# A new order of batch loads in a fused sparse-attention and feed-forward kernel

## The chip, the core and the metric

The kernel runs on one core of a Trainium2 chip. The metric is the device time of one execution in microseconds. Before the change it is 222.42 us, the median of three runs (220.64 to 222.76). Less is better. A result counts as faster or slower here if it differs by over 2%.

Five engines work side by side: TensorE (PE, matmuls, with its weight loads listed apart as PEld), VectorE (DVE), ScalarE (ACT), GpSimd (POOL) and SyncE (SP). In this kernel GpSimd issues the loads that change the type from f32 to bf16 or f16, and SyncE issues the stores and the transposes made by DMA. Matmul results lie in PSUM, everything else on chip in SBUF.

## The reference

Two parts, one after the other. The first is attention with 4 batches, 8 heads, 768 positions and head size 64. Each query sees the keys within 15 positions of it (`window`), and one summary for each block of 32 positions: the maximum of the block's keys, with the mean of its values.

```python
k_sum = k.reshape(B, H, nb, block, D).max(axis=3)
v_sum = v.reshape(B, H, nb, block, D).mean(axis=3)
scores_l = scale * np.matmul(q, k.transpose(0, 1, 3, 2))     # kept where |i - j| < 16
scores_s = scale * np.einsum('bhsd,bhnd->bhsn', q, k_sum) + np.log(block)
# softmax over both kinds of scores together: a
attn = np.matmul(a, np.concatenate([v, v_sum], axis=2))
# ... (cut: mask, softmax)
x = attn.transpose(0, 2, 1, 3).reshape(B * S, H * D)          # 3072 x 512
h = x @ w_in                                                  # 512 x 2048
out = (h / (1.0 + np.exp(-1.702 * h))) @ w_out                # 2048 x 512
```

## The kernel before

The feed-forward part is cut into eight *units* of 384 rows, two for each batch: unit u holds half u % 2 of batch u // 2. A unit has an *input stage* (`ff_in`: 16 tiles `nt` of 4 matmuls each, then the gelu on ScalarE) and an *output stage*. Units 0 and 1 have an output stage of their own (`ff_out`). Units 2 and 3, 4 and 5, 6 and 7 are taken as pairs: two input stages, then one output stage for both, in which the products `a`, `b`, `c` with parts 1 to 7 save one multiplication in eight. The attention of the next batch is slipped in between these matmuls.

The helpers that matter here (cuts are marked):

```python
def load_kc(b):                       # load_qc(b) is the same for q
    rows["k", b] = rows_tile("k", b)  # tile kb, or for batch 2 a half of kq; queries: qb, kq
    cast_load(k, b, rows["k", b])     # 8 DMAs on GpSimd's queue, one a head

def load_vc(b):                       # vw[b % 2] is used by every second batch
    w5 = vw[b % 2].rearrange("p (j e) h c -> p j e h c", e=2)
    for j in range(NJ):               # NJ = 6 DMAs on GpSimd's queue
        pool.dma_start(out=w5[:, j, 0, :, 0:D], in_=...)

def v_odd(b): ...                     # VectorE: 4 copies of the value rows within vw
def vsum(s, js): ...                  # 24 matmuls ps_vs<-vw,E: sums over value blocks
def block_sums(): ...                 # VectorE: 4 copies vs<-ps_vs
def halo_dmas(w5, j0): ...            # 4 DMAs vw<-vw on GpSimd's queue: neighbours' rows
def sum_dmas(w5, j0, eng=pool): ...   # 2 DMAs vw<-vs: the block sums to each tile

def tk(p, s):                         # keys of batch 1, two heads: transposed on TensorE
    ps = trans(rows["k", 1][:, p].rearrange("p j h d -> p j (h d)"))   # 6 matmuls ps_t<-ident,kb
    copy(act if p % 2 else dve, at(flat_kx(p, s), 0, [[256, NJ], [192, 2], [1, 64]]),
         ps.rearrange("p (j e c) -> p j e c", e=2, c=64))
    ks = attp.tile([128, nb], BF16, name="ks", tag="ks")
    dve.tensor_reduce(out=ks, in_=ps.rearrange("p (n s) -> p n s", s=block),
                      axis=AX.X, op=ALU.max)
    key_halos(p, s)
    key_rows(p, s, ks)

def xk(g, b): ...                     # SyncE: 2 DMA transposes, keys of 4 heads, batches 2 and 3
def xq(g, b): ...                     # SyncE: 1 DMA transpose, queries of 4 heads, batches 2 and 3
def dx(g, m): ...                     # SyncE: 1 DMA transpose xT<-x of an attention result
```

The transposes and block sums (`ps_t`, `ps_vs`), and also the scores `ps_s`, share one PSUM pool of two buffers. The pool `mm` of four banks holds the rest.

Units 0 and 1 (their input stages, and what is put beside them):

```python
for u in range(2):
    todo = {}
    if u == 0:
        # ... (cut: casts of the queries of batch 0)
    else:
        def value_rows():
            vsum(1, range(NJ))
            block_sums()
            halo_dmas(w51, 0)
            sum_dmas(w51, 0)
            load_kc(2)
            load_qc(2)
            load_vc(2)

        todo = {1: [lambda: tk(0, 1)], 2: [lambda: v_odd(1)], 4: [lambda: tk(1, 1)],
                6: [value_rows, lambda: tk(2, 1)], 8: [lambda: tk(3, 1)]}
        ff_in(u, range(3))
    for nt in range(0 if u else N0, NT):
        if u == 0 or nt > 2:
            ff_in(u, (nt,))
        for f in todo.get(nt, ()):
            f()
    exp_soon()
    if u == 0:
        beside(1, -1)
        load_qc(1)
        busy(6)
    # ... (cut: order of the output stage)
    for i, (ms, part) in enumerate(order):
        ff_out(u, ms, part)
        beside(u + 1, i)              # attention of the next half batch
        # ... (cut)
        if u == 1 and i == 3:
            for g in range(2):
                xk(g, 2)
```

The pairs of units, with what is put into their input stages (`first` for unit 2b, `second` for unit 2b + 1):

```python
for b in range(1, B):
    n, s = b + 1, (b + 1) % 2
    more = n < B
    ss = stage.tile([128, NP - 1, 2, NI, 128], F16, name="ss", tag="vf")
    u = 2 * b
    # ... (cut: pairs "a", "b", "c", whose sums go to ss[:, 0], ss[:, 1], ss[:, 2])
    first, second = {}, {0: [lambda: pairs["a"].sums(0, NI)]}
    for nt, i0, i1 in ((7, 0, 4), (13, 4, 7)):
        second[nt] = [lambda i0=i0, i1=i1: pairs["b"].sums(i0, i1),
                      lambda i0=i0, i1=i1: pairs["c"].sums(i0, i1)]
    if b == 1:
        first = {0: [lambda: values(1, 1, 0, True)],
                 2: [lambda: dx(0, 1), lambda: values(1, 1, 1, True)], 4: [lambda: dx(1, 1)]}
    elif more:
        for g in range(2):
            xk(g, n)
    if more:
        first.setdefault(6, []).append(lambda: v_odd(n))
        # ... (cut: rest_k, maxima and halos of the keys of batch n, at nt 3, 5, 8, 10)
        def bring():
            w5 = vw[s].rearrange("p (j e) h c -> p j e h c", e=2)
            vsum(s, range(NJ))
            block_sums()
            halo_dmas(w5, 0)
            sum_dmas(w5, 0)
            if n + 1 < B:
                load_kc(n + 1)
                load_vc(n + 1)
                load_qc(n + 1)

        when = 7 if b == 1 else 14
        first.setdefault(when, []).append(lambda: [xq(g, n) for g in range(2)])
        first.setdefault(9 if b == 1 else 15, []).append(bring)
    for w, todo in ((u, first), (u + 1, second)):
        ff_in(w, range(3))
        # ... (cut: the other tiles, and after each what todo has for it)
    # ... (cut: the output stage of the pair, with the attention of batch n)
```

Batch 0 comes in another way and is over early. Each engine carries out its instructions in the order of the program.

Of the kernel before, what the change touches and what calls it, by code (L numbers as in the profile page):

```python
# [11 lines left out]
F16 = mybir.dt.float16  # L12
# [23 lines left out]
def kernel(  # L36
# [10 lines left out]
    B, H, S, D = q.shape  # L47
# [8 lines left out]
    NJ = S // 128  # L56
# [8 lines left out]
    dve = _Ordered(tc, nc.vector)  # L65
    act = _Ordered(tc, nc.scalar)
    pool = _Ordered(tc, nc.gpsimd)
    sp = _Ordered(tc, nc.sync)

    consts = ctx.enter_context(tc.tile_pool(name="consts", bufs=1))  # L70
# [44 lines left out]
    def cast_load(x, b, dst):  # L115

        for h in range(H):
            pool.dma_start(out=dst[:, h // 2, :, h % 2],
                           in_=x[b, h].rearrange("(j p) d -> p j d", p=128))

    def rows_tile(what, b):
        if b != 2:
            return castp2.tile([128, NP, NJ, 2, D], BF16, name=what + "b", tag=what + "b")
        if "two" not in early:
            early["two"] = stage.tile([128, 2, NP, NJ, 2, D], BF16, name="kq", tag="kf")
        return early["two"][:, "kq".index(what)]

    def load_kc(b):
        rows["k", b] = rows_tile("k", b)
        cast_load(k, b, rows["k", b])  # L130

    def load_qc(b):
        rows["q", b] = rows_tile("q", b)
        cast_load(q, b, rows["q", b])

    def load_vc(b):
        w5 = vw[b % 2].rearrange("p (j e) h c -> p j e h c", e=2)
        for j in range(NJ):
            pool.dma_start(out=w5[:, j, 0, :, 0:D],
                           in_=v[b, :, j * 128:(j + 1) * 128].rearrange("h p d -> p h d"))  # L140

    def v_odd(b):
        for p in range(NP):
            r = rows_of(b % 2, p)
            dve.tensor_copy(out=r[:, :, 1], in_=r[:, :, 0])
# [129 lines left out]
    def copy(eng, out, in_):  # L275
        if eng is act:
            act.activation(out=out, in_=in_, func=ACT.Copy)
        elif eng == "dve_alone":

            dve.tensor_reduce(out=out, in_=in_.unsqueeze(len(in_.shape)), axis=AX.X, op=ALU.max)  # L280
        else:
            eng.tensor_copy(out=out, in_=in_)
# [24 lines left out]
    def rows_of(s, p, hh=None):  # L307

        hs = slice(2 * p, 2 * p + 2) if hh is None else slice(2 * p + hh, 2 * p + hh + 1)
        return vw[s].rearrange("p (j e) h c -> p j e h c", e=2)[:, :, :, hs, 0:D]  # L310
# [24 lines left out]
    def busy(n):  # L335
        ps = pmm.tile([128, 512], F32, name="ps_w", tag="mm")
        for i in range(n):
            pe.matmul(out=ps[:, 0:128], lhsT=warm[:, 0:128], rhs=warm[:, 0:128],
                      start=True, stop=True)
# [8 lines left out]
    def halo_dmas(w5, j0):  # L348
        halo_odd(w5, j0)
        halo_even(w5, j0)  # L350
# [26 lines left out]
    def at(ap, start, dims):  # L377
        a = ap[:, start:start + 1]
        return bass.AP(tensor=a.tensor, offset=a.offset, ap=[a.ap[0]] + dims)

    def flat_kx(p, s):
        return kx[p][s].rearrange("p t c -> p (t c)")
# [182 lines left out]
    def trans(src):  # L565
        big = psb.tile([128, 2048], BF16, name="ps_t", tag="big")
        for j in range(NJ):
            pe.transpose(out=big[:, j * 128:(j + 1) * 128], in_=src[:, j], identity=ident)
        return big[:, 0:S]

    def tk(p, s):
        ps = trans(rows["k", 1][:, p].rearrange("p j h d -> p j (h d)"))
        copy(act if p % 2 else dve, at(flat_kx(p, s), 0, [[256, NJ], [192, 2], [1, 64]]),
             ps.rearrange("p (j e c) -> p j e c", e=2, c=64))
        ks = attp.tile([128, nb], BF16, name="ks", tag="ks")
        dve.tensor_reduce(out=ks, in_=ps.rearrange("p (n s) -> p n s", s=block),
# [3 lines that stand above are left out]
# [221 lines left out]
            self.store(1, 0, True)  # L801

    gate = consts.tile([128, 2], F32, name="gate")
    dve.memset(gate, 0.0)

    def gelu_soon():
# [161 lines left out]
# [3 lines that stand above are left out]
            for p in range(NP):  # L971
                todo.setdefault(12 + p // 2, []).append(lambda p=p: cast_q(dve, p, 1))
# [3 lines that stand above are left out]
                block_sums()  # L976
                halo_dmas(w51, 0)
                sum_dmas(w51, 0)
                load_kc(2)
                load_qc(2)  # L980
                load_vc(2)

            todo = {1: [lambda: tk(0, 1)], 2: [lambda: v_odd(1)], 4: [lambda: tk(1, 1)],
                    6: [value_rows, lambda: tk(2, 1)], 8: [lambda: tk(3, 1)]}
            ff_in(u, range(3))
        for nt in range(0 if u else N0, NT):
            if u == 0 or nt > 2:
# [4 lines that stand above are left out]
        if u == 0:  # L992
            beside(1, -1)
            load_qc(1)
            busy(6)
        order = [(ms, part) for ms in range(JH) for part in range(4)]
        if u == 0:

            order = [(ms, part) for part in range(4) for ms in range(JH)]
        for i, (ms, part) in enumerate(order):  # L1000
            ff_out(u, ms, part)
            beside(u + 1, i)
            if u == 0 and i in (4, 7, 10):
                w_sums(i // 3 - 1)
            if u == 1 and i == 2:
                w_sums(3)
# [3 lines that stand above are left out]
# [19 lines left out]
# [5 lines that stand above are left out]
        pairs = {"a": Pair((u, 0), (u, 1), ss[:, 0], not more),  # L1034
                 "b": Pair((u, 2), (u + 1, 2), ss[:, 1], not more),
                 "c": Pair((u + 1, 0), (u + 1, 1), ss[:, 2], not more)}
# [5 lines that stand above are left out]
            first = {0: [lambda: values(1, 1, 0, True)], 2: [lambda: dx(0, 1), lambda: values(1, 1, 1, True)],  # L1042
                     4: [lambda: dx(1, 1)]}
# [5 lines that stand above are left out]
            at_k = [(first, 3), (first, 5), (first, 8), (first, 10)] if b == 1 else \  # L1049
                [(first, 8), (first, 10), (first, 12), (first, 14)]  # L1050
            for p, (when, nt) in enumerate(at_k):
                when.setdefault(nt, []).append(lambda p=p: rest_k(p, s))
# [4 lines that stand above are left out]
                block_sums()  # L1057
                halo_dmas(w5, 0)
                sum_dmas(w5, 0)
                if n + 1 < B:  # L1060
                    load_kc(n + 1)
                    load_vc(n + 1)
                    load_qc(n + 1)

            when = 7 if b == 1 else 14
            first.setdefault(when, []).append(lambda: [xq(g, n) for g in range(2)])
            first.setdefault(9 if b == 1 else 15, []).append(bring)
        for w, todo in ((u, first), (u + 1, second)):
            ff_in(w, range(3))
            for nt in range(NT):  # L1070
                if nt > 2:
                    ff_in(w, (nt,))
                for f in todo.get(nt, ()):
                    f()
        pairs["a"].p1(act)
        if more:
            exp_soon()
        for m in "bc":
            pairs[m].sums(NI - 1, NI)
        for what in order:  # L1080
            getattr(pairs[what[0]], "p" + what[1])()
            if more:
                for it in meet.get(what, ()):
                    attend(n, it)
# [30 lines left out]
```

## Time and profile before

| | |
|---|---|
| time, median of three runs | 222.42 us (220.64 to 222.76) |
| span of the profiled execution | 222.2 us |
| TensorE busy | 203.3 us, 92% of the span |
| VectorE, ScalarE, GpSimd busy | 133.5, 123.3, 94.0 us |
| loads and copies issued by GpSimd: share of 16 DMA engines over the span | 75.3% |
| DMAs issued by SyncE, same share | 29.7% |
| packets under 512 B | 84480 of 96609 |

How to read it: "PE ps_vs L28 <- DMA vw<-in_v_dram" says that TensorE's instruction writing `ps_vs` waited for a load that writes `vw` from the input `v`. Line 28 is a helper through which every instruction passes, so lines are told apart by their tiles. Here is the part of the page that shows the span in 40 slices of 5.55 us each. A digit is the busy share of an engine in tenths, or the clock granted to TensorE in tenths:

```profile
PE   7779998997999994179999999999999999999994
PEld 2556554555655562036688886655888866568883
DVE  6687936788818774075466776089677740347332
ACT  2675775446675593017782456767824567773220
POOL 8779988698699830049995001022000000000000
PEclk9999999999999999559999999999999999999999
DMA  6999999999999999969999345799013460000223
```

The kernel starts with the first half of batch 0. Units 0 and 1 last until 77.8 us, units 2 and 3 with their pair's output stage until 135, units 4 and 5 until 180, and units 6 and 7 until the end. The sixteenth to eighteenth slices, 83 to 100 us, are in unit 2.

The waits with the largest totals in the stretch from 76 to 114 us are, in us in total, how often, and the longest:

```profile
ACT gT L28 <- PE ph L28: 16.9, 24, 11.4
POOL vw L28 <- DVE vw L28: 16.7, 1, 16.7
PEld L28 <- issue: 12.4, 19, 2.5
DVE vw L28 <- DMA vw<-in_v_dram: 10.0, 1, 10.0
PE ps_vs L28 <- DMA vw<-in_v_dram: 8.9, 5, 2.4
```

### The profile page before, as it was taken

To read this page: it belongs to the slowest core of one execution; us is meant where nothing else is said; L and a number is where in the kernel's file an instruction comes from. 1 tells how busy PE (TensorE), PEld (TensorE's weight loads), DVE (VectorE), ACT (ScalarE), POOL (GpSimd) and SP (SyncE) were. 2 spreads that over 40 slices of the span, in tenths; PEclk is the share of its full clock that TensorE was granted. 3 is DMA by queue.
4 is the path that set the end of the run, shared out by engine and by line. 5 is a ranking of instruction groups with operands and counts; after the bars stand their busy time and mean duration, and the time that the engine had idled before them with its cause. 6 is when DMAs were issued, how large, how long until landed. Compare 5 with 4: busy or idle time off the path is not lost.

```text
span 222.2 us, 5497 instructions
## 1 busy us (share of the span) xinstructions
PE 203.3 (92%) x2193; PEld 137.0 (62%) x2193; DVE 133.5 (60%) x392; ACT 123.3 (55%) x230; POOL 94.0 (42%) x172
## 2 busy tenths in 40 slices
PE   7779998997999994179999999999999999999994
PEld 2556554555655562036688886655888866568883
DVE  6687936788818774075466776089677740347332
ACT  2675775446675593017782456767824567773220
POOL 8779988698699830049995001022000000000000
PEclk9999999999999999559999999999999999999999
DMA  6999999999999999969999345799013460000223
GB/s 181 272 170 182 258 230 214 159 169 213 172 108 153 144 118 207 148 91 145 126 145 149 95 114 176 132 124 165 0 39 97 112 185 1 0 3 24 74 71 118
DMA packets 96609, 29.33 MB, mean 132 GB/s; under 512 B 84480, under 2 KB 93600, under 8 KB 96584
## 3 DMA queue, kind: packets, MB, share of 16 engines
q0 software_dynamic: 67920, 14.88, 75.3%
q1 hardware_dynamic: 28664, 14.11, 29.7%
q8 instruction: 17, 0.28, 0.5%
q14 instruction: 8, 0.07, 0.1%
HBM read 27.26 MB, written 6.29 MB: 151 GB/s over the span
## 4 chain that ended last, share of the span: by engine, by line
PE 57%; DMA 27%; POOL 9%; DVE 2%; issue 1%; SPq 1%; ACT 1%; POOLq 0%
PE ph L28 26%; PE px L28 14%; DMA w_out_sb<-in_moe_w_out_dram 8%; PE pw L28 7%; DMA vw<-in_v_dram 7%; POOL kq L28 4%; DMA kq<-in_q_dram 4%; PE py L28 4%; DMA qb<-in_q_dram 3%; DMA kb<-in_k_dram 3%; POOL qb L28 3%; PE ps_av L28 2%; PE ps_s L28 2%; DMA kf<-in_k_dram 2%; POOL vw L28 1%
## 5 line engine op out<-in xcount | busy, mean ns | idle before, releaser
L28 PE MATMUL ph<-xT,w_in_sb 128*128 128x384 f16 x512 | 87.5, 330 | 0.0
L28 ACT ACTIVATE gT<-ph 128x384 f16<-128x384 f32 x128 | 60.9, 490 | 37.3 <-PE ph L28 37.0
L28 PEld LDWEIGHTS <-w_in_sb 128*128 128x128 f16 x512 | 50.1, 99 | 33.3 <-issue 2.1
L28 PEld LDWEIGHTS <-gT 128*128 128x128 f16 x384 | 35.7, 98 | 12.3
L28 ACT ACTIVATE a_sb<-ps_s 128x768 bf16<-128x768 f32 x28 | 21.2, 806 | 12.0 <-PE ps_s L28 11.9
L28 POOL DMA_DIRECT2D vw<-vw x12 | 6.6, 553 | 43.4 <-DVE vw L28 35.5
L28 PE MATMUL po<-w_out_sb,gT 128*128 128x512 f16 x96 | 23.1, 380 | 0.0
L28 PEld LDWEIGHTS <-ss 128*128 128x128 f16 x216 | 21.0, 98 | 2.5
L28 DVE TENSOR_TENSOR a_sb<-a_sb,mk 128x768 bf16<-128x768 bf16 x28 | 15.5, 554 | 9.9 <-ACT a_sb L28 8.4
L28 DVE TENSOR_TENSOR ss<-gT 128x512 f16<-128x512 f16 (+3 forms) x21 | 8.0, 382 | 21.5 <-ACT gT L28 21.5
L28 ACT ACTIVATE t<-px 128x256 f32<-128x256 f32 x21 | 8.1, 384 | 20.2 <-PE px L28 20.2
L28 PE MATMUL pw<-tb,gT 128*128 128x256 f16 x144 | 18.7, 273 | 0.0
L28 PE MATMUL px<-ta,ss 128*128 128x256 f16 x144 | 18.7, 273 | 0.0
L28 POOL DMA_DIRECT2D vw<-in_v_dram x18 | 16.0, 945 | 2.0 <-DMA kq<-in_q_dram 2.0
L28 DVE TENSOR_TENSOR x<-ps_av,rc 128x384 f16<-128x384 f32 x28 | 15.6, 558 | 1.0
L28 DVE TENSOR_REDUCE ks<-kx 128x24 bf16<-128x768 bf16 x12 | 11.3, 945 | 7.6 <-DMA kx<-kb 7.6
L28 POOL DMA_DIRECT2D kb<-in_k_dram x16 | 13.3, 869 | 2.7 <-DMA w_out_sb<-in_moe_w_out_dram 2.7
L28 ACT ACT_TABLE_LOAD x10 | 12.8, 1283 | 1.0 <-PEq L1099 0.8
L28 POOL DMA_DIRECT2D qb<-in_q_dram x16 | 13.3, 950 | 0.0
L28 DVE TENSOR_TENSOR osb<-pw,t 128x256 f32<-128x256 f32 x18 | 7.6, 423 | 9.2 <-PE pw L28 5.1
L28 PE MATMUL ps_vs<-vw,E 128*32 128x128 bf16 x72 | 2.6, 232 | 8.9 <-DMA vw<-in_v_dram 8.9
L28 DVE COPY vw<-vw 128x768 bf16<-128x768 bf16 x12 | 4.3, 419 | 10.0 <-DMA vw<-in_v_dram 10.0
(103 smaller groups left out, 256.4 us busy)
## 6 DMA issues: line engine op xcount, KB each, us to landing
out_dram<-osb SPq DMA_DIRECT2D x18, 256.0 KB, 3.1
vw<-in_v_dram POOLq DMA_DIRECT2D x18, 128.0 KB, 5.0
w_in_sb<-in_moe_w_in_dram POOLq DMA_DIRECT2D x4, 512.0 KB, 9.5
w_out_sb<-in_moe_w_out_dram POOLq DMA_DIRECT2D x4, 512.0 KB, 17.7
kf<-in_k_dram SPq DMA_DIRECT2D x8, 192.0 KB, 3.7
kb<-in_k_dram POOLq DMA_DIRECT2D x16, 96.0 KB, 5.3
qb<-in_q_dram POOLq DMA_DIRECT2D x16, 96.0 KB, 5.4
out_dram<-osb SPq DMA_DIRECT2D x12, 128.0 KB, 1.7
```

The source lines that it names most:

```text
L28: r = f(*a, **kw)
```

## The change

The loads on GpSimd's queue are put in another order, and the work that needs them in unit 1 as well.

- The keys of batch 2 are issued straight after the queries of batch 1, ahead of the value rows of batch 1 (its halo copies and block sums within `vw`). They no longer stand behind VectorE's work on these values.
- After the value rows of batch 1 come the values of batch 2, and then its queries. Before, it was keys, queries, values.
- In unit 1 the work on the keys and values of batch 1 is set to other tiles: the first two keys ahead of the value copies, the block sums at tile 9 where they were at tile 6. The copies of the transposed keys out of PSUM are all on VectorE, where two of four were on ScalarE.
- The loads of batch 3 follow a small GpSimd copy that reads a part of `ss`, which VectorE writes at tile 7 of unit 3. So they are held until then. Before, they went out once the value rows of batch 2 were issued.

The amount of data loaded and the number of matmuls stay the same.

```diff
--- before.py
+++ after.py
@@ -570,7 +570,7 @@
 
     def tk(p, s):
         ps = trans(rows["k", 1][:, p].rearrange("p j h d -> p j (h d)"))
-        copy(act if p % 2 else dve, at(flat_kx(p, s), 0, [[256, NJ], [192, 2], [1, 64]]),
+        copy(dve, at(flat_kx(p, s), 0, [[256, NJ], [192, 2], [1, 64]]),
              ps.rearrange("p (j e c) -> p j e c", e=2, c=64))
         ks = attp.tile([128, nb], BF16, name="ks", tag="ks")
         dve.tensor_reduce(out=ks, in_=ps.rearrange("p (n s) -> p n s", s=block),
@@ -801,6 +801,7 @@
             self.store(1, 0, True)
 
     gate = consts.tile([128, 2], F32, name="gate")
+    after = consts.tile([128, 2], F16, name="after")
     dve.memset(gate, 0.0)
 
     def gelu_soon():
@@ -976,12 +977,11 @@
                 block_sums()
                 halo_dmas(w51, 0)
                 sum_dmas(w51, 0)
-                load_kc(2)
+                load_vc(2)
                 load_qc(2)
-                load_vc(2)
-
-            todo = {1: [lambda: tk(0, 1)], 2: [lambda: v_odd(1)], 4: [lambda: tk(1, 1)],
-                    6: [value_rows, lambda: tk(2, 1)], 8: [lambda: tk(3, 1)]}
+
+            todo = {0: [lambda: tk(0, 1)], 3: [lambda: tk(1, 1)], 5: [lambda: v_odd(1)],
+                    6: [lambda: tk(2, 1)], 9: [value_rows], 11: [lambda: tk(3, 1)]}
             ff_in(u, range(3))
         for nt in range(0 if u else N0, NT):
             if u == 0 or nt > 2:
@@ -992,6 +992,7 @@
         if u == 0:
             beside(1, -1)
             load_qc(1)
+            load_kc(2)
             busy(6)
         order = [(ms, part) for ms in range(JH) for part in range(4)]
         if u == 0:
@@ -1057,11 +1058,15 @@
                 block_sums()
                 halo_dmas(w5, 0)
                 sum_dmas(w5, 0)
-                if n + 1 < B:
-                    load_kc(n + 1)
-                    load_vc(n + 1)
-                    load_qc(n + 1)
-
+
+            def later():
+                pool.tensor_copy(out=after, in_=ss[:, 2, 0, 0, 0:2])
+                load_kc(n + 1)
+                load_vc(n + 1)
+                load_qc(n + 1)
+
+            if n + 1 < B:
+                second[7].append(later)
             when = 7 if b == 1 else 14
             first.setdefault(when, []).append(lambda: [xq(g, n) for g in range(2)])
             first.setdefault(9 if b == 1 else 15, []).append(bring)
```

## The prediction

> **What bounds the kernel now.** I read the 40 slices of the page first, then the chain of waits from 60 us on, then TensorE's own timeline around the hole that both show, then the stretches with granted clock, then the timelines of VectorE, GpSimd and the sync queue to see why the data came when it did. The chain:
>
> ```profile
> 53.39 7.45 DMA qb<-in_q_dram
> 60.84 0.28 issue
> 61.12 8.95 POOL kq L28 x11
> 70.07 8.58 DMA kq<-in_q_dram
> 78.65 0.30 issue
> 78.95 0.86 POOL vw L28
> 79.81 15.83 DMA vw<-in_v_dram
> 95.64 0.04 issue
> 95.68 0.30 PE ps_vs L28 x4
> 95.98 16.19 PE ph L28 x88
> ```
>
> Start, length, what. From 53 to 95.7 us the end is set by loads alone: queries of batch 1 (qb), keys and queries of batch 2 (kq), then values of batch 2 (vw). From 95.98 the rest of the chain is TensorE without a gap until 218.94, followed by the last addition and store. So whatever is taken out ahead of 95.98 comes off the time, as long as no later wait opens. TensorE's timeline (start, length, instruction, idle before and who ended it):
>
> ```profile
> 80.77 4.72 PE L28 MATMUL ph<-xT,w_in_sb 128*128 128x384 f16 x28
> 85.42 0.24 PE L28 MATMUL ps_vs<-vw,E 128*32 128x128 bf16 x4
> 86.09 0.24 PE L28 MATMUL ps_vs<-vw,E 128*32 128x128 bf16 x4 [0.43 <-DMA vw<-in_v_dram]
> 88.68 0.24 PE L28 MATMUL ps_vs<-vw,E 128*32 128x128 bf16 x4 [2.35 <-DMA vw<-in_v_dram]
> 91.19 0.30 PE L28 MATMUL ps_vs<-vw,E 128*32 128x128 bf16 x4 [2.27 <-DMA vw<-in_v_dram]
> 93.63 0.30 PE L28 MATMUL ps_vs<-vw,E 128*32 128x128 bf16 x4 [2.14 <-DMA vw<-in_v_dram]
> 95.68 0.30 PE L28 MATMUL ps_vs<-vw,E 128*32 128x128 bf16 x4 [1.75 <-DMA vw<-in_v_dram]
> ```
>
> The 24 block-sum matmuls of batch 2 follow the six value loads one by one, 2.0 to 2.6 us apart, from 85.42 to 95.98 us: 10.6 us for work that took 0.52 us for batch 1 (53.90). The stretches (busy us and count of TensorE, its weight loads, VectorE, ScalarE, GpSimd; then clock, DMA share, GB/s) show what comes after the hole:
>
> ```profile
> 85.00:90.00 5.00, 1.14 (x16) 0.41 (x14) 0.95 (x5) 0.86 (x2) 0.00 (x0) 0.93 1.74 179
> 90.00:95.00 5.00, 0.59 (x8) 0.22 (x8) 0.00 (x0) 0.00 (x0) 0.00 (x0) 0.50 1.48 142
> 95.00:100.00 5.00, 4.32 (x19) 2.11 (x19) 4.00 (x14) 1.12 (x3) 2.37 (x5) 0.54 0.58 92
> 100.00:105.00 5.00, 5.00 (x32) 3.01 (x31) 2.78 (x8) 3.56 (x8) 5.00 (x7) 1.00 1.09 143
> ```
>
> The clock is halved from about 89 us and stays so until nearly 100, so the first matmuls after the hole run slowly. A second, small hole:
>
> ```profile
> 55.71 0.49 PE L28 MATMUL ps_t<-ident,kb 128*128 128x128 bf16 x6 [1.29 <-DVE ks L28]
> ```
>
> In unit 1's input stage the third key transpose waits for a PSUM buffer, because VectorE reads the second key's maximum only after four value copies (1.95 us from 52.84).
>
> **What the Trainium skill says.** "TensorE: Matmul & The Clock Gate", Part 1 (The HAM clock gate), says that TensorE's clock drops to half after an idle window of about 3.4 us and comes back after about as long a busy one. The trace agrees: 0.93, 0.50, 0.54, 1.00 above. "DMA: Bandwidth & Descriptors", Issuing engines are not separate DMA queues, says that transfers of all issuing engines run on the same 16 DMA engines and interleave; its section Queues, rings and completion order says each DMA engine takes turns between the queues. The trace agrees: one value load of batch 2 landed every 2.0 to 2.6 us while the sync queue ran transposes and stores; those of batch 3, with the sync queue idle, landed 3.9 to 4.5 us after issues 0.87 us apart.
>
> **The change, part by part.** GpSimd's order of issue was qb(1), value rows(1), k2, q2, v2. It becomes qb(1), k2, value rows(1), v2, q2. ("Value rows" are the four halo copies and two sum copies inside vw.)
>
> *k2.* GpSimd ends qb(1) at 54.37 and then waits for VectorE, issues the six row copies and waits 1.00 us for a landing; k2 goes out from 59.26 to 66.89. Now it starts at 54.4, 8 issues of 0.85 us, the last held to about 61 by the landing of the last qb at 60.84: done at about 62. Its landing (3.3 us after issue) moves from 69.3 to about 65.5.
>
> *Value rows(1).* Issued 62 to about 65.7 (2.27 + 1.38 us as now), landing 3 to 4 us later, 68.5 to 69.5; now 62.8 (58.6 + 4.2). First reader: the value product of batch 1 at 70.27, about 69.1 after the shift below. Touch and go: I put down 0.2 us.
>
> *v2 ahead of q2.* v2 is issued from about 65.7 and takes the place that q2 has now, beside the key transposes. q2's last load was issued at 72.5 and landed 9.4 us later, 81.9. v2 moves the same bytes (6 x 128 KB for 8 x 96 KB) and starts some 1 to 2 us earlier: landed at about 80. It is needed at about 84 (85.42 less the shift). The hole closes: end of the sums 95.98 becomes 85.42 + 0.45, so 10.1 us less.
>
> *Clock.* 64 ph matmuls at full clock took 10.40 us (135.30 in the chain), 0.1625 each. The 88 after the hole took 16.19, at that rate 14.30: 1.9 us less.
>
> *Unit 1.* Keys go in pairs ahead of the value copies, and all four PSUM copies are on VectorE: 2 x 0.56 us more there, 2 x 0.81 less on ScalarE. One key is 0.56 + 0.95 + 0.37 + 0.23 = 2.1 us; four keys, value copies 1.95 and sums 1.17 make 11.5 from 51.1: 62.6 if simply added, about 61.5 with the overlaps that the timeline shows (now 60.4). TensorE's stage is 64 x 0.1625 + 4 x 0.35 + 0.45 = 12.3 from 48.6: 60.9, now 62.2. The 1.29 goes, some 0.2 may come back on the fourth transpose: 1.1 less.
>
> *What opens.* Unit 3 needs xT of batch 1, second half. Its two transposes were issued at 82.0 and 83.4 and landed 7.9 and 8.5 us later (89.9 and 91.9), behind the key transposes and two stores of 10 us; hidden today by the hole. Now unit 3 starts at 77.83 - 1.1 + 10.4 + 0.95 + 0.45 = 88.5, and wants the second xT about 1 us into its first group. With issue 1.1 earlier and a little less traffic they land at about 88.5 and 90.5: 1.0 us of wait.
>
> *q2 last.* It takes v2's place, without the query transposes beside it: landed at about 91. The two qT transposes follow it (7.5 and 7.1 us to landing for batch 3): 95 and about 98. Unit 3 ends at 88.5 + 1.0 + 10.4 = 99.9, and the first score of batch 2 comes two products (1.74) later at 101.6, needing only the first. No wait.
>
> *Batch 3.* The held loads go out from about 95 (after tile nt 7 of unit 3) instead of 101.0, and are done by about 116; batch 3 is first read in the transposes at 138 (about 126 after). Nothing on the path, bar a slower xT transpose or two.
>
> Sum: 10.1 + 1.9 + 1.1 - 0.2 - 1.0 = 11.9 us. From 222.42: 210.5. I add 0.5 for waits that I have not seen: 211.0.
>
> **The rivals.** *Rows late:* k2 ahead of the rows delays batch 1's value product. For it: both sit on one queue and the margin is near zero. Against: the row copies queue up behind nothing but k2, which is nearly through by then; today they are issued behind the whole of qb and still land 4.2 to 6.0 us later. Two more us: 213. *xT wait in full:* if the sync queue is no faster than now, unit 3 waits until 91.9, 2.4 us more than my 1.0 leaves: 213.5. If it waits over 3.4 us the clock falls too and 2 us more go: 215.5. *Query wait:* if q2 is slow in landing, the score at 101.6 waits for its transposes; if they take as long as now (10.9 us) from 91, that is 102, hardly a wait; at 95 it is 4 to 5 us: 215.5. *Only moved:* v2 still late by half: 217. Against it: an earlier issue by some 8 us.
>
> **Range and chances.** The steps that save are read from holes in the trace and are nearly certain; those that cost are 0 to 3 us each and unlikely to come together. The three times before spread by 2.1 us. Range 208.5 to 215.5. Two per cent is below 218.0: it takes two rivals at once to miss it, hence 0.91 faster, 0.07 same, 0.02 slower.
>
> **What would show it.** In TensorE's timeline the six ps_vs groups of batch 2 should be one block of about 0.5 us near 84, with no wait for vw; the clock should be 1.00 throughout 85 to 105; the ps_t wait on DVE ks gone. A wait of about 1 us for xT should stand at the start of unit 3. Wrong if a wait for vw stands at the value product near 69, if a wait of over 2 us stands before ps_s near 101, or if the block sums still wait.

## The result, and the profile after

| | before | after |
|---|---|---|
| time, median | 221.62 us | 212.37 us (211.98 to 213.9) |
| ratio to before | | 0.959, 95% interval 0.952 to 0.967 |
| span of the profiled execution | 222.2 us | 210.6 us |
| TensorE busy | 203.3 us, 92% | 201.3 us, 96% |

The change makes the kernel 4.1% faster. First the slices of the page of the changed kernel, two rows of them, TensorE's busy share and its granted clock:

```profile
PE   7879999999999999989999989999999999999993
PEclk9999999999999999999999999999999999999999
```

The hole of slices 16 to 18 is gone, and with it the two slices at half clock. In place of the hole stand two dents of one tenth. What they are is seen in the chain of waits of the changed kernel (start, length, what):

```profile
79.30 2.60 PE ph L28 x16
81.90 8.32 DMA xT<-x
90.22 0.04 issue
90.27 9.59 PE ph L28 x58
99.85 0.87 PE px L28 x8
```

Before, three loads in a row set the end up to 95.7 us. Now the chain is TensorE's, but for the DMA transpose of an attention result (xT) in unit 3. A second one of the same kind stands in unit 4. TensorE's timeline of the changed kernel:

```profile
83.89 0.52 PE L28 MATMUL ps_vs<-vw,E 128*32 128x128 bf16 x24
84.34 5.05 PE L28 MATMUL ph<-xT,w_in_sb 128*128 128x384 f16 x30
90.27 9.59 PE L28 MATMUL ph<-xT,w_in_sb 128*128 128x384 f16 x58 [0.88 <-DMA xT<-x]
...
124.60 9.59 PE L28 MATMUL ph<-xT,w_in_sb 128*128 128x384 f16 x58 [0.64 <-DMA xT<-x]
```

The 24 block sums are one block of 0.52 us, where they were six groups over 10.6 us. The stretches (busy us and count of TensorE, weight loads, VectorE, ScalarE, GpSimd; clock, DMA share, GB/s) have the clock at 1.00 throughout:

```profile
85.00:90.00 5.00, 4.39 (x28) 2.48 (x26) 4.92 (x19) 2.94 (x6) 2.26 (x4) 1.00 1.82 159
90.00:95.00 5.00, 4.73 (x30) 2.85 (x30) 1.16 (x2) 3.53 (x8) 1.24 (x2) 1.00 1.31 135
95.00:100.00 5.00, 5.00 (x33) 3.11 (x32) 3.14 (x9) 3.72 (x9) 2.78 (x4) 1.00 1.21 121
```

From TensorE's timeline one can read where each stage begins: the first `ph` of an input stage, the first `po` or `px` of an output stage. This table has the lengths of the stages, worked out so for every profile of this study. The stages left out are equal to 0.1 us in all of them (23.13 for the output stage of units 2 and 3, 65.67 from the output stage of units 4 and 5 to the end).

| kernel, lengths in us | unit 1 begins at | unit 1 input | unit 1 output | units 2, 3 input | units 4, 5 input | sum of the four |
|---|---|---|---|---|---|---|
| before | 48.59 | 13.64 | 15.61 | 34.17 | 21.35 | 84.77 |
| before, second profile | 48.15 | 13.72 | 15.61 | 34.10 | 21.36 | 84.79 |
| changed | 48.19 | 12.29 | 15.82 | 23.39 | 22.16 | 73.66 |
| changed, second profile | 49.46 | 12.29 | 17.20 | 23.44 | 22.11 | 75.04 |
| changed, third profile | 49.48 | 14.17 | 15.61 | 22.35 | 21.88 | 74.01 |
| values ahead of queries alone | 48.18 | 13.52 | 15.61 | 22.69 | 21.35 | 73.17 |
| keys early alone | 49.95 | 13.90 | 15.61 | 24.06 | 21.35 | 74.92 |
| unit 1 alone | 48.34 | 12.30 | 15.61 | 37.15 | 21.35 | 86.41 |
| changed, old unit 1 | 49.34 | 14.15 | 15.61 | 23.08 | 21.36 | 74.20 |
| changed, no hold | 49.61 | 12.70 | 15.61 | 22.35 | 21.38 | 72.04 |
| changed, xT on TensorE | 49.62 | 12.34 | 15.61 | 23.87 | 21.54 | 73.36 |
| changed, transposes split | 49.17 | 12.59 | 15.61 | 22.35 | 21.49 | 72.04 |
| changed, rows between | 48.78 | 12.41 | 15.61 | 24.23 | 21.45 | 73.70 |
| all three | 49.41 | 12.30 | 15.61 | 22.71 | 21.35 | 71.97 |

The shortest of each column, 12.29 + 15.61 + 22.35 + 21.35 = 71.60, is about what these stages take when TensorE waits for nothing. I call it the floor. Before was 13.2 us above it, and the changed kernel is 2.1 to 3.4 above it. The begin of unit 1 varies by 1.8 us between executions, so stage lengths are a safer measure than spans.

### The profile page after: what moved, and what is told of

It reads as the page before. It is cut to its first block, busy times and chain, and to the rows that moved or that the text cites. A ratio compares the mean times of both kernels' runs of the same rounds, so it can differ in the third digit from the quotient of the medians.

```text
span 210.6 us, 5499 instructions
## 1 busy us (share of the span) xinstructions
PE 201.3 (96%) x2193; PEld 137.1 (65%) x2193; DVE 133.0 (63%) x394; ACT 122.0 (58%) x228; POOL 95.0 (45%) x173
## 3 DMA queue, kind: packets, MB, share of 16 engines
q0 software_dynamic: 67920, 14.88, 81.9%
## 4 chain that ended last, share of the span: by engine, by line
PE 81%; DMA 10%; DVE 3%; POOL 2%; issue 1%; SPq 0%
PE ph L28 36%; PE px L28 14%; PE po L28 10%; DMA xT<-x 8%; PE pw L28 7%; PE ps_av L28 4%; PE py L28 3%; PE ps_s L28 3%; DMA kf<-in_k_dram 2%; POOL vb L28 2%; DVE qT L28 1%; PE ps_t L28 1%; PE ps_x L28 1%; PE ps_q L28 1%; DVE x_sb L28 1%
## 5 line engine op out<-in xcount | busy, mean ns | idle before, releaser
L28 PE MATMUL ph<-xT,w_in_sb 128*128 128x384 f16 x512 | 86.2, 326 | 1.6 <-DMA xT<-x 1.5
L28 PEld LDWEIGHTS <-w_in_sb 128*128 128x128 f16 x512 | 49.4, 98 | 34.0 <-issue 2.2
L28 POOL DMA_DIRECT2D kb<-in_k_dram x16 | 13.2, 863 | 2.0 <-DMA w_out_sb<-in_moe_w_out_dram 1.6
L28 ACT ACTIVATE osb<-px 128x256 f32<-128x256 f32 x9 | 3.4, 379 | 12.0 <-PE px L28 12.0
L28 DVE RECIPROCAL rc<-ps_av 128x6 f32<-128x6 f32 x32 | 6.0, 188 | 6.6 <-PE ps_av L28 6.3
```

The lines of the kernel that those rows point to most:

```text
L28: r = f(*a, **kw)
```

## The experiments

Theory A was that the values' place in the queue made the gain, theory B that the earlier start of the keys did. The first four runs took the parts of the change one by one, on the kernel before, each timed in three rounds (on this chip before took 221.56 us). Times are medians of all executions; the ratios and their intervals leave out the executions that are over 1.5% above the fastest of the same kernel, so that a gain by the ratio can be up to 1.3 us smaller than one by the medians.

**Values ahead of queries, alone.**

```diff
                 load_kc(2)
-                load_qc(2)
                 load_vc(2)
+                load_qc(2)
```

> The kernel before with one edit: the values of batch 2 are loaded ahead of its queries (keys, values, queries), everything else as before, so the keys still go out behind batch 1's value rows. Theory A (the place of the values in the queue made the gain): the values now land where the queries did, at about 82 us, before the block sums want them at 85.4; the hole of 10 us and the 1.9 us at half clock go, a wait of 1 to 2 us for xT opens at unit 3. Time 9.0 to 10.5 us below before, nearly the whole gain of the change. Theory B (the earlier start of the keys made it): the values still land after 85.4 by some us, the hole shrinks by half at most, gain 3 to 6 us.

Measured: 213.2 us, ratio 0.968 (0.959 to 0.977), so 8.4 us less by the medians and 7.1 by the ratio. TensorE's timeline of this kernel:

```profile
84.90 0.52 PE L28 MATMUL ps_vs<-vw,E 128*32 128x128 bf16 x24
85.35 5.05 PE L28 MATMUL ph<-xT,w_in_sb 128*128 128x384 f16 x30
90.58 2.60 PE L28 MATMUL ph<-xT,w_in_sb 128*128 128x384 f16 x15 [0.17 <-DMA xT<-x]
```

The block sums don't wait. The last value load was issued at 70.1 and landed 8.9 us later, at 79.0; the sums want it at 84.9. This one swap closes the whole hole. The gain lies between the 9.0 that A put as its least and the 6 that B put as its most, but the profile is A's: nothing waits for the values. The wait for xT is 0.17, not 1 to 2. The four stages of the table sum to 73.17 us here, less than in any of the three profiles of the changed kernel (73.66 to 75.04), and the changed kernel's three medians (212.37 to 213.92) lie on both sides of 213.2. So no run shows that the other parts of the change add to the gain.

**Keys early, alone.**

```diff
             load_qc(1)
+            load_kc(2)
             busy(6)
...
-                load_kc(2)
                 load_qc(2)
                 load_vc(2)
```

> The kernel before with one edit: the keys of batch 2 are issued straight after the queries of batch 1, ahead of batch 1's value rows; then queries and values of batch 2 in the old order. Theory A: the queue only gets some 2 to 4 us ahead, the values still come last and land at 92 to 94 us instead of 95.6, the block sums still wait 6 to 8 us: gain 1.5 to 4 us. Theory B: most of the gain, 7 us or more.

Measured: 216.02 us, ratio 0.979 (0.968 to 0.989), so 5.5 us less by the medians and 4.8 by the ratio; whether it is over 2% stays open. Both theories miss: A put at most 4, B at least 7. In the profile five of six value loads are there in time (TensorE's timeline):

```profile
87.06 0.46 PE L28 MATMUL ps_vs<-vw,E 128*32 128x128 bf16 x20
89.05 0.24 PE L28 MATMUL ps_vs<-vw,E 128*32 128x128 bf16 x4 [1.53 <-DMA vw<-in_v_dram]
```

A had moved the values' landing by no more than their issue. The landings, issue plus time to landing, show why that is too little. In this run the first five query loads landed between 68.3 and 71.4 us, one each 0.8 us. SyncE's key transposes began at 70.2. The six value loads then landed between 78.5 and 89.0, one each 2.1 us. In the kernel before, where the transposes began at 68.57, none of the query loads had landed by then: they came between 71.1 and 81.9, one each 1.5 us, and the values between 83.5 and 95.6, one each 2.4 us. The values of batch 3 in the kernel before, with SyncE's queue idle, landed one each 1.0 us (111.5 to 116.3). So a load that lands before the transposes begin takes about half of the time of one of the same size that lands beside them and the stores that follow them. An issue 4.1 us earlier (75.7 for 79.8) brought a landing 6.6 us earlier. This fits that either edit closes most of the hole, and that both together are not the sum of the two.

**Unit 1 alone.** The edit is the two hunks of the change that touch `tk` and `todo`; the loads stay in their old order at the end of `value_rows`.

> The kernel before with only the rework of unit 1 (all four key copies on VectorE, other tiles for keys, value copies and block sums). Both theories: the 1.29 us wait of the third key transpose goes and unit 1's input stage is 1.1 to 1.4 us shorter, but the loads of batch 2 still set the end of the hole, and batch 1's value rows go out about 1 us later, so the hole grows by as much: time the same within 0.5 us, at most 1.5 us more. A third theory, C (each us of TensorE's stage counts by itself), says 1.1 to 1.4 us less.

Measured: 224.33 us, ratio 1.018 (1.008 to 1.028), so 2.8 us more by the medians and 3.9 by the ratio; the four stages of its profile are 1.6 longer together. The stage became 1.34 shorter as expected. TensorE's timeline, first and last group of the block sums:

```profile
87.59 0.30 PE L28 MATMUL ps_vs<-vw,E 128*32 128x128 bf16 x4 [3.69 <-DMA vw<-in_v_dram]
...
97.03 0.30 PE L28 MATMUL ps_vs<-vw,E 128*32 128x128 bf16 x4 [1.05 <-DMA vw<-in_v_dram]
```

The values land at 97.0 (issued 81.3, 15.7 to landing), 1.4 later than before, while TensorE is there 1.5 us sooner. Two things fit: the keys are issued from 60.6 us instead of 59.3, and with TensorE ahead the first store of unit 1 and the key transposes behind it come at 67.0 instead of 68.6, so more of the loads lie beside transposes. Theory C falls, and the others' bound of 1.5 us more is passed.

**The kernel before, once more.**

> The kernel before, unchanged, for a second profile. The first one's execution took 224.23 us, 2.6 above the median of the timed runs of before, 221.62. If the length of the hole differs from execution to execution with the landing of the values, a second profile of about 221 to 222 us shows a hole shorter by 1 to 3 us and stages otherwise equal to 0.3 us. If the difference lies elsewhere, the hole is 10.2 us again.

Measured: 221.89 us, ratio 0.999 (0.995 to 1.004). The profiled execution took 223.81 us, and its stages are those of the first profile (34.10 for 34.17). The hole is as long in both. But this profile too fell on one of the longest executions (the twenty took 218.48 to 223.97), so whether the hole is shorter in the quicker ones stays open. The clocks on record speak for it: nine of the twenty executions have a mean granted clock of 0.984 or more, and their median is 220.7 us; the other eleven, the profiled one with 0.977 among them, have 222.6. So the quicker executions spend less time at half clock in the mean.

The next four ran on the changed kernel, in five rounds (before on these chips: 222.65 us). Theory D was that SyncE's chain of key transposes, stores and xT transposes is now the limit, and that it moves little with TensorE.

**The changed kernel, once more.**

> The changed kernel, unchanged, beside its variants. The block sums of batch 2 in one block of 0.5 us, a wait for the second xT of 0.5 to 1.5 us in unit 3 and one of 0.3 to 1 us in unit 4; time 211.5 to 213.

Measured: 213.92 us, ratio 0.963 (0.956 to 0.970), 0.9 above the range expected. Besides the two waits for xT (0.93 and 0.59) TensorE's timeline has a third:

```profile
70.29 0.19 PE L28 MATMUL ps_av<-vw,a_sb 128*64 128x65 bf16 x1 [0.42 <-DMA vw<-vs]
71.42 0.54 PE L28 MATMUL ps_av<-vw,a_sb 128*64 128x65 bf16 x23 [0.94 <-DMA vw<-vs]
```

These are batch 1's value rows, late behind the keys of batch 2. The last block-sum copy was issued at 67.3 here and at 65.0 in the first profile, where it landed at 68.6 just as the product wanted it. This is the rival "rows late". Of the three profiles of the changed kernel it costs 0.2 us in the first, 1.6 in this one and nothing in the third.

**Old unit 1 on the changed kernel.** The same two hunks undone.

> The changed kernel with unit 1 as it was before (two key copies on ScalarE, old tiles). Theory D (the next limit is the sync queue's chain of key transposes, stores and xT, whose end at about 90.2 to 90.5 us hardly moves with TensorE): the 1.29 us wait of the third key transpose comes back, but the xT wait of 0.88 us in unit 3 shrinks to 0.2 or nothing; time 0.2 to 0.6 us above the changed kernel. Theory C (TensorE's stage counts by itself): 1.1 to 1.4 us above.

Measured: 213.36 us, ratio 0.962 (0.956 to 0.969). No difference from the changed kernel beside it can be measured, which is against C. The profile has unit 1 at 14.15, with the transpose waiting 1.51 for VectorE again. In return the wait for the value rows is nothing, and units 4 and 5 are at their shortest. The wait for xT is gone, as D has it, but TensorE now waits 0.56 us in unit 3 for a gelu result of ScalarE, so units 2 and 3 are only 0.36 shorter than in the second profile.

**No hold on batch 3.**

```diff
             def later():
-                pool.tensor_copy(out=after, in_=ss[:, 2, 0, 0, 0:2])
                 load_kc(n + 1)
```

> The changed kernel without the small copy that holds the loads of batch 3: they go out some 5 us earlier, behind the value rows of batch 2. Theory D: the loads end near 120 instead of 124.7 us, ahead of unit 4's xT transposes, so unit 4's wait of 0.64 us goes; the query transposes land a little later but ahead of the score that wants them: 0.4 to 0.8 us below the changed kernel. Rival (the hold is what keeps the queries of batch 2 in time): a wait for qT opens before the first score of batch 2 near 101 us, 0.5 to 3 us above.

Measured: 213.16 us, ratio 0.963 (0.956 to 0.969). Unit 4 no longer waits (21.38 for 22.11), as D has it. But the loads didn't end near 120: the last one landed at 124.6. The second query transpose took 14.2 us to landing instead of 8.2, at 104.2, still without a wait. By medians this is 0.8 less than the changed kernel, within the intervals. The rival, a wait for queries, doesn't show. That the hold makes the wait in unit 4 isn't shown either: with the hold, units 4 and 5 take 21.88 to 22.16 in the three profiles of the changed kernel, but 21.36 to 21.54 in four variants that keep it (old unit 1, and three below). What the hold buys doesn't show.

**Second xT on TensorE.**

```diff
-                     4: [lambda: dx(1, 1)]}
+                     4: [lambda: tx(1, 1)]}
```

> The changed kernel with the second xT of batch 1 transposed on TensorE (6 matmuls, 0.34 us, and one VectorE copy of 0.55 us) instead of by DMA: takes away the suspected wait of unit 3. Theory D: the 0.88 us wait goes, 0.34 us of TensorE comes, unit 4's wait may grow as TensorE comes earlier: 0 to 0.6 us below the changed kernel. Rival (the wait is covered elsewhere, VectorE gets the copy late): same or up to 0.5 us above.

Measured: 213.85 us, ratio 0.965 (0.959 to 0.970): nothing gained. The wait is exchanged for another (TensorE's timeline):

```profile
82.46 0.34 PE L28 MATMUL ps_x<-identx,x 128*128 128x128 f16 x3 [0.49 <-DVE x L28]
83.15 0.34 PE L28 MATMUL ps_x<-identx,x 128*128 128x128 f16 x3 [0.35 <-DVE x L28]
```

TensorE comes to the transposes before VectorE has normalized the rows. With the DMA transpose that time was hidden.

The last four ran on one chip in five rounds (before: 221.71 us): the changed kernel and three versions meant to remove its waits.

**The changed kernel, third time.**

> The changed kernel unchanged, as the measure for its three variants on the same chip. Time 212 to 214; the wait for xT in unit 3 of 0.5 to 1.5 us again, and in some executions a wait of up to 1.4 us for batch 1's value rows at its first value product (seen in one of two profiles).

Measured: 213.03 us, ratio 0.965 (0.959 to 0.970). Here neither the rows nor unit 3's xT are waited for, but unit 1 is long: the fourth key transpose waits 1.72 us for VectorE. VectorE's timeline shows what held it:

```profile
55.93 3.32 DVE L28 COPY vw<-vw 128x768 bf16<-128x768 bf16 x4
```

In the first profile of the changed kernel the same four copies are:

```profile
54.48 1.16 DVE L28 COPY vw<-vw 128x768 bf16<-128x768 bf16 x4
```

They took 0.87 to 0.90 us each here and 0.35 there. GpSimd issued key loads through all of them here, without a pause from 53.22 to 59.89. In the first profile it stood still, waiting for a landing, until 55.32, while most of these copies ran. The Trainium skill says in "SBUF — State Buffer", SBUF: two separate sides, that a VectorE operation in a two-port mode and a GpSimd operation hold a shared pair of ports as an exclusive lock: the one that starts first has it for the whole instruction, and the other waits. The lengths agree with that, if these copies run in such a mode, which no trace shows; a run that sets it apart was not made.

**Key transposes split.** SyncE's transposes of the keys of heads 4 to 7 go behind the two xT transposes.

```diff
             if u == 1 and i == 3:
-                for g in range(2):
-                    xk(g, 2)
+                xk(0, 2)
...
-                     4: [lambda: dx(1, 1)]}
+                     4: [lambda: dx(1, 1), lambda: xk(1, 2)]}
...
-            at_k = [(first, 3), (first, 5), (first, 8), (first, 10)] if b == 1 else \
+            at_k = [(first, 3), (first, 5), (second, 1), (second, 3)] if b == 1 else \
```

> The changed kernel with the key transposes of heads 4 to 7 of batch 2 moved behind the two xT transposes on the sync queue (and what reads them to unit 3). Theory D (the key transposes slow the loads beside them and hold up xT behind them): the stores and xT land some 5 us earlier, at 84 to 87 us, the loads of batch 2 land faster, unit 3 starts without a wait: 0.5 to 1.2 us below the changed kernel. Rival (total DMA work sets it, the order in the queue doesn't matter; the late keys or queries are missed): xT not before 89 us, or a new wait for keys or queries near 100 us, same or up to 2 us above.

Measured: 210.8 us, ratio to before 0.955 (0.950 to 0.960). That is 2.2 us (1.0%) less than the changed kernel on the same chip, more than expected, though the two intervals still touch. SyncE's timeline, first in the first profile of the changed kernel, then in this one:

```profile
66.83 9.09 SPq L28 DMA_TRANSPOSE kx<-kq  x4
76.01 1.05 SPq L28 DMA_DIRECT2D out_dram<-osb  x2
80.51 3.23 SPq L28 DMA_TRANSPOSE xT<-x  x2
```

```profile
68.10 3.83 SPq L28 DMA_TRANSPOSE kx<-kq  x2
72.72 4.92 SPq L28 DMA_DIRECT2D out_dram<-osb  x2
81.58 3.30 SPq L28 DMA_TRANSPOSE xT<-x  x2
85.06 2.88 SPq L28 DMA_TRANSPOSE kx<-kq  x2
```

xT took 4.9 and 4.2 us to landing, at 86.5 and 87.2, where the first profile of the changed kernel has 7.7 and 8.3 (88.2 and 90.2). The last query load landed at 85.7 instead of 93.1. Unit 3 starts without a wait, and units 2 and 3 are at their shortest. That is what D says: the key transposes delay what is beside them and behind them. But the changed kernel's own profile on this chip, the third, has 5.9 and 5.2 for xT (89.4 and 90.1), 88.8 for the last query load, and units 2 and 3 just as short. The 2.0 us between the two stage sums (74.01 and 72.04) lie in unit 1 and in units 4 and 5, which the split doesn't touch. So the split makes the landings earlier, but that this is where its gain comes from isn't shown.

**Rows between the keys.** The first four key loads go ahead of batch 1's value rows, the other four behind them.

```diff
             load_qc(1)
-            load_kc(2)
+            load_kc(2, range(4))
...
                 sum_dmas(w51, 0)
+                load_kc(2, range(4, 8))
                 load_vc(2)
```

> The changed kernel with batch 1's value rows between the fourth and the fifth key load of batch 2 instead of behind the eighth. If the rows behind eight loads cost time in some executions, they now land some 3 us earlier and the wait at the first value product is always 0; in executions that did not wait nothing changes: 0 to 0.8 us below the changed kernel, with the slowest executions nearer to the fastest. Rival: GpSimd waits for VectorE between the loads and the values of batch 2 come later: same or slower.

Measured: 213.01 us, ratio 0.965 (0.960 to 0.971), the same as the changed kernel. The rows landed at 65.4 instead of 68.6 and nothing waited for them. The profiled execution had 1.46 us of wait for xT. The third profile of the changed kernel has neither wait, so what the edit exchanged for what isn't shown.

**All three.** Both edits, and no hold.

> Both edits of the two variants before and no hold on the loads of batch 3. If all three waits (rows, xT in unit 3, xT in unit 4) are independent and go, 1.2 to 2.5 us below the changed kernel, profile near 209 us; if they hide one another or the total DMA work sets the time, within 0.5 us of it.

Measured: 212.35 us, ratio 0.961 (0.955 to 0.966), 0.7 below the changed kernel. Its profile has the shortest stages of all, 0.37 above the floor, yet its time is 1.5 above the version with the split alone (0.44 above the floor). The profiles don't tell why: the two profiled executions are only 0.5 us apart (212.26 and 211.73). Without the hold the second query transpose took 12.7 us (landed at 104.8); but it took 14.2 in the version that has only the hold taken out, and that one was no slower than the changed kernel beside it (213.16 and 213.92).

## Why the prediction was right, step by step

| step of the prediction | put down | measured in the first profile |
|---|---|---|
| hole of the block sums and half clock | 10.1 + 1.9 less | units 2 and 3 shorter by 10.78 with the new wait, 11.7 without it |
| unit 1's input stage | 1.1 less | 1.35 less |
| rows of batch 1 late | 0.2 more | 0.21 more |
| wait for xT in unit 3 | 1.0 more | 0.88 more |
| unit 4 and batch 3's loads | nothing | 0.81 more |
| begin of unit 1 | same | 0.40 less, within its spread of 1.8 |
| sum | 11.9 less | 11.5 less (222.16 to 210.64) |

**The hole** was read rightly as the whole matter. The values landed at 82.7 us and not at 80, with 1.2 us to spare and not 4. But the reason was narrower than told. The swap alone gave 8.4 us by the medians, where the whole change gave 9.25, and its profile is the shorter one. The prediction took the early keys as a part of the gain; they are worth 5.5 us alone, but beside the swap no gain from them shows.

**Unit 1** was right in its stage in two of three profiles (in the third the stage is 14.17) and wrong as a separate term. Alone it makes the kernel 2.8 us slower, and taken out of the changed kernel it makes no difference that can be measured. A TensorE stage that ends in a wait for a load isn't worth its length.

**Rows late** was rightly called touch and go: 0.2 us in the first profile, 1.6 in the second (17.20 for 15.61), nothing in the third. That the first profile has just the 0.2 put down is luck; in the second stands the wait at the value product that the prediction named as a sign of being wrong, and the gain was there all the same.

**xT** was right in time and size in the first profile: 88.2 and 90.2 against 88.5 and 90.5. The wait is 0.93 in the second and gone in the third.

**Queries last** was right in that nothing waits. The margin was smaller than put down: the first transpose landed at 97.8 and not 95, 3.7 us ahead of the score.

**Batch 3** is a term that failed. "Nothing on the path" stood on loads that end at about 116. They were held until 97.7 and ended at 124.7, beside the transposes of unit 4, which waited 0.64. Without the hold that wait is gone, but in four variants that keep it units 4 and 5 take 21.36 to 21.54 us against its 21.38, so what makes the wait stays open.

**The base** is the other mis-sized term. The sum was read from a profiled execution of 224.23 us and taken off a median of 222.42. The profiles differ by 11.5 us, the timed medians by 9.25, since before's profiled executions lie 1.9 to 2.6 us above its medians and the changed kernel's 0.3 to 1.2. Before's executions spread over 6 us (218.2 to 224.6), and both its profiles fell near the upper end; whether that is chance stays open.

## What to carry to other kernels

Order the loads of one queue by when they are wanted, and look at what another queue does meanwhile: here a load that landed before the other queue's transposes began took about half of the time of one that landed beside them. A wait that a chain of loads sets isn't shortened by a faster engine ahead of it: it got 3.0 us longer here when unit 1 became 1.3 us shorter. Even with the loads no longer last, the gain in unit 1 didn't show in the time (213.92 us with it, 213.36 without). And when a change has several parts, run each alone: here one swap of two lines does what the whole change does. When such a hole is closed, waits come up that were hidden behind it, and it is best to list their landing times in the same profile before expecting the whole hole back.

## What was unexpected of the hardware

Beside DMA transposes on SyncE's queue and the stores behind them, loads on GpSimd's queue landed one each 1.5 us (96 KB) and 2.1 to 2.4 us (128 KB); without them it was 0.8 us (96 KB) and 1.0 us (128 KB). Stores of 256 KB behind these transposes took 8.4 to 10.6 us to landing, and the one just ahead of them 3.0 to 3.2. And VectorE's copies of 128x768 in SBUF took 0.35 us each in one profile, where GpSimd mostly stood still, and 0.87 to 0.90 in another, where it issued loads all the while.
